# Three stores of the last batch issued as partition halves, and the fallback code's transfers moved to GpSimd

## The chip, the cores and the metric

The kernel runs on one core of one Trainium2 chip. The metric is device time in microseconds (us). The four runs of the kernel before lie within half a per cent of their median, and all its fast runs on record between 133.78 and 136.07 us; each run is labelled fast or slow state, and comparisons below use fast runs. "Span" is the time from the first to the last instruction of the one profiled execution; it is shorter than the device time of the same execution: by 2.0 us for the kernel before (132.8 against 134.76 us).

Engine names as in the profile: PE is TensorE, DVE is VectorE, ACT is ScalarE, POOL is GpSimd, SP is SyncE. SP does no arithmetic here; it issues the stores and the first load. SBUF is the core's on-chip memory, where tiles lie in 128 partitions; HBM is the main memory, where x and the output lie. The page counts 16 DMA engines and the packets that they carry (5666 in the kernel before). Each of the last batch's 1 MB stores has 16 completions in the trace, one for each engine as they are read here (127.98 to 131.62 us for the last store); a store is said to have landed with its last completion.

## The reference, cut to what matters

```python
def _attn_ref(x, inducing):            # x: 4 x 12480 x 128 fp32, inducing: 32 x 128
    ...
    h = mab(I, x)                      # 32 inducing points attend to all rows of a batch
    return mab(x, h)                   # all rows attend to the 32 results

def _moe_ref(x, w_in, w_out):          # w_in: 128 x 2048, w_out: 2048 x 128
    h = x @ w_in
    g = 0.5 * h * (1.0 + erf(h * inv_sqrt2))
    return (g @ w_out)                 # 49920 x 128 fp32
```

Only the traffic matters: about 25.6 MB of x are read and 25.6 MB of output are written, once each.

## The kernel before

The kernel runs a fast path that is valid for inputs in a certain range, counts range checks, and at the very end branches to a slow `general` code if any check failed. For the inputs the flag is zero, so `general` is never run, though its instructions are in the program.

The output rows are laid out so that each SBUF partition holds neighbouring rows. A store therefore moves one long contiguous piece per partition. In batches 0 to 2 two units share one tile and one store of 2 MB. In the last batch (`b = 3`) each unit is stored alone: 128 partitions x 16 rows x 512 bytes, that is 8 KB per partition and 1 MB in all. There are six such stores and one small tail store.

```python
APART = 3
...
    def rows_of(self, t):
        t0 = self.b * N + self.pair * 2 * SGT
        t = t[t0 : t0 + self.held * self.p, :]
        return t.rearrange("(p c) d -> p c d", p=self.p)
...
        # in b_inverse: the tile that the output of a unit is written to
        elif u.b >= APART:
            o = sb.tile([128, 32, 128], FP16, tag="xh", bufs=XBUFS)
            o = o.rearrange("p c d -> p (c d)").bitcast(FP32)
            o = o.rearrange("p (c d) -> p c d", d=128)
...
    def b_store(bt, u, alone):
        if alone:
            c0, c1, o = u.c_pair, u.c_pair + u.nc, bt.live[("o", u.idx)]
        else:
            c0, c1, o = 0, u.held, bt.live[("pair", u.pair)]
        nc.sync.dma_start(out=u.rows_of(out)[:, c0:c1, :], in_=o)
...
    with tc.If(flag > 0, preferred_fallthrough_block=False):
        general(tc, x, moe_w_in, moe_w_out, out, ind_s, identity)
```

Of the kernel before, what the change touches and what calls it, by code (L numbers as in the profile page):

```python
# [15 lines left out]
B = 4  # L16
N = 12480
# [221 lines left out]
def kernel(  # L239
# [8 lines left out]
    nc = tc.nc  # L248
# [61 lines left out]
    for j in range(4):  # L310
# [3 lines left out]
        out=stack4,  # L314
        in_=identity.rearrange("p (j m) -> p m j", j=4),
# [5 lines left out]
        out=same_m, in_=stack4.unsqueeze(1).broadcast_to([128, 4, M])  # L321
# [386 lines left out]
    def b_store(bt, u, alone):  # L708
        if alone:
            c0, c1, o = u.c_pair, u.c_pair + u.nc, bt.live[("o", u.idx)]  # L710
        else:
            c0, c1, o = 0, u.held, bt.live[("pair", u.pair)]
        nc.sync.dma_start(out=u.rows_of(out)[:, c0:c1, :], in_=o)

    checked = []

    def check_total():
# [27 lines left out]
            o=OBUFS,  # L745
# [120 lines left out]
    for k, u in enumerate(order):  # L866
# [59 lines left out]
        if u.last or alone:  # L926
            stored = plan.add(
                key(6),
                {"SP": 0.4},
                lambda e, bt=bt, u=u, alone=alone: b_store(bt, u, alone),  # L930
                scaled,
                gives=o_given,
                move=part(u, STORE_US) * (1 if alone else 2),
            )
# [29 lines left out]
        out=failed,  # L964
# [11 lines left out]
    with tc.If(flag > 0, preferred_fallthrough_block=False):  # L976
        general(tc, x, moe_w_in, moe_w_out, out, ind_s, identity)
# [4 lines left out]
def general(tc, x, moe_w_in, moe_w_out, out, ind_s, identity):  # L982

    nc = tc.nc
    T = 96
    with (
        tc.tile_pool(name="g_w", bufs=1) as gw,
        tc.tile_pool(name="g_sb", bufs=2) as gs,
        tc.tile_pool(name="g_ps", bufs=1, space=bass.MemoryType.PSUM) as gp,
    ):  # L990
        w_in = gw.tile([128, DFF], FP32)
        nc.sync.dma_start(out=w_in, in_=moe_w_in)
        w_out = gw.tile([128, NBLK, 128], FP32)
        nc.sync.dma_start(
            out=w_out, in_=moe_w_out.rearrange("(blk p) d -> p blk d", p=128)
        )
        iT = gw.tile([C, M], FP32)
        mx = gw.tile([M, 1], FP32)
        r = gw.tile([M, 1], FP32)
        rr = gw.tile([M, 1], FP32)  # L1000
        h = gw.tile([M, C], FP32)
        hn = gw.tile([M, C], FP32)
        hT = gw.tile([C, M], FP32)

        def transpose_to(dst, src, rows):
            tp = gp.tile([128, 128], FP32, tag="tp")
            n = src.shape[1]
            nc.tensor.transpose(tp[:n, :rows], src, identity[:rows, :rows])
            nc.vector.tensor_copy(out=dst, in_=tp[:n, :rows])

        transpose_to(iT, ind_s, M)
        nc.vector.memset(r, 1.0)
        nc.vector.memset(h, 0.0)
        xf = x.rearrange("b n d -> (b n) d")



        with tc.For_i(0, 2 * B, 1) as turn:
            nc.vector.tensor_scalar(
                out=rr, in0=r, scalar1=1e-9, scalar2=None, op0=ALU.add  # L1020
            )
            nc.vector.reciprocal(out=rr, in_=rr)
            nc.vector.tensor_scalar(
                out=hn, in0=h, scalar1=rr, scalar2=None, op0=ALU.mult
            )
            transpose_to(hT, hn, M)
            nc.vector.memset(mx, -3.0e38)
            nc.vector.memset(r, 0.0)
            nc.vector.memset(h, 0.0)
            base = (turn >> 1).with_bounds(min_val=0, max_val=B - 1) * N  # L1030
            with tc.For_i(0, N, T) as t:
                xg = gs.tile([T, C], FP32, tag="xg")
                nc.sync.dma_start(out=xg, in_=xf[bass.ds(base + t, T), :])
                xTg = gs.tile([C, T], FP32, tag="xTg")
                transpose_to(xTg, xg, T)

                s1 = gp.tile([M, T], FP32, tag="s1")
                nc.tensor.matmul(s1, iT, xTg, start=True, stop=True)
                tm = gs.tile([M, 1], FP32, tag="tm")
                nc.vector.tensor_reduce(out=tm, in_=s1, axis=AX.X, op=ALU.max)  # L1040
                nc.vector.tensor_tensor(out=tm, in0=mx, in1=tm, op=ALU.max)
                nm = gs.tile([M, 1], FP32, tag="nm")
                nc.vector.tensor_scalar(
                    out=nm, in0=tm, scalar1=-SCALE, scalar2=None, op0=ALU.mult
                )
                fall = gs.tile([M, 1], FP32, tag="fall")
                nc.scalar.activation(
                    out=fall, in_=mx, func=AF.Exp, bias=nm, scale=SCALE
                )
                nc.vector.tensor_copy(out=mx, in_=tm)  # L1050
                e = gs.tile([M, T], FP32, tag="e")
                re = gs.tile([M, 1], FP32, tag="re")
                nc.scalar.activation(
                    out=e, in_=s1, func=AF.Exp, bias=nm, scale=SCALE, accum_out=re
                )
                nc.vector.scalar_tensor_tensor(
                    out=r, in0=r, scalar=fall, in1=re, op0=ALU.mult, op1=ALU.add
                )
                eT = gs.tile([T, M], FP32, tag="eT")
                transpose_to(eT, e, M)  # L1060
                hp = gp.tile([M, C], FP32, tag="hp")
                nc.tensor.matmul(hp, eT, xg, start=True, stop=True)
                nc.vector.scalar_tensor_tensor(
                    out=h, in0=h, scalar=fall, in1=hp, op0=ALU.mult, op1=ALU.add
                )

                s2 = gp.tile([T, M], FP32, tag="s1")
                nc.tensor.matmul(s2, xTg, hT, start=True, stop=True)
                nm2 = gs.tile([T, 1], FP32, tag="nm2")
                nc.vector.tensor_reduce(out=nm2, in_=s2, axis=AX.X, op=ALU.max)  # L1070
                nc.vector.tensor_scalar(
                    out=nm2, in0=nm2, scalar1=-SCALE, scalar2=None, op0=ALU.mult
                )
                a = gs.tile([T, M], FP32, tag="a")
                ra = gs.tile([T, 1], FP32, tag="ra")
                nc.scalar.activation(
                    out=a, in_=s2, func=AF.Exp, bias=nm2, scale=SCALE, accum_out=ra
                )
                nc.vector.tensor_scalar(
                    out=ra, in0=ra, scalar1=1e-9, scalar2=None, op0=ALU.add  # L1080
                )
                nc.vector.reciprocal(out=ra, in_=ra)
                nc.vector.tensor_scalar(
                    out=a, in0=a, scalar1=ra, scalar2=None, op0=ALU.mult
                )
                aT = gs.tile([M, T], FP32, tag="aT")
                transpose_to(aT, a, T)
                y_ps = gp.tile([C, T], FP32, tag="y")
                nc.tensor.matmul(y_ps, hn, aT, start=True, stop=True)
                y = gs.tile([C, T], FP32, tag="ysb")  # L1090
                nc.vector.tensor_copy(out=y, in_=y_ps)
                z = gp.tile([128, NBLK // 4, 4, 128], FP32, tag="z")
                g = gs.tile([128, NBLK // 4, 4, T], FP32, tag="g")
                for blk in range(NBLK):
                    zb = z[:, blk // 4, blk % 4, :T]
                    nc.tensor.matmul(
                        zb,
                        w_in[:, blk * 128 : (blk + 1) * 128],
                        y,
                        start=True,  # L1100
                        stop=True,
                    )
                nc.scalar.activation(out=g, in_=z[:, :, :, :T], func=AF.Gelu)
                o_ps = gp.tile([T, 128], FP32, tag="hp")
                for blk in range(NBLK):
                    nc.tensor.matmul(
                        o_ps,
                        g[:, blk // 4, blk % 4, :],
                        w_out[:, blk, :],
                        start=(blk == 0),  # L1110
                        stop=(blk == NBLK - 1),
                    )
                og = gs.tile([T, 128], FP32, tag="og")
                nc.vector.tensor_copy(out=og, in_=o_ps)
                nc.sync.dma_start(out=out[bass.ds(base + t, T), :], in_=og)


# [28 lines left out]
```

## Time and profile before

| | kernel before |
|---|---|
| time, median of 4 runs | 134.35 us (133.78 to 134.8) |
| span of the profiled execution | 132.8 us |
| share of 16 DMA engines: loads (q0) and stores (q1) | 49.5 % + 48.3 % |
| DMA rate from 114 to 126 us | 418 to 430 GB/s |
| mean duration of an 8 KB store packet, from 112 to 128 us, by the microsecond in which it starts | 0.309 to 0.312 us |
| last store: issued, first and last of its 16 completions | 122.60, 127.98, 131.62 us |

The first lines are from the page of the kernel before: the span; then, over 40 equal slices of the span (3.3 us each), the busy share of the 16 DMA engines in tenths and the rate that they moved; then the queues with packets, MB and share of the engines' time; last the issues of the six 1 MB stores, with the size in KB and the median time from issue to landing in us.

```profile
span 132.8 us, 3490 instructions
...
DMA  4999999999999999999999999999999999999970
GB/s 123 302 223 215 217 200 220 212 220 210 220 205 220 215 200 313 333 398 367 299 318 348 266 227 324 321 412 425 430 423 426 415 437 413 411 434 425 421 300 15
DMA packets 5666, 40.17 MB, mean 303 GB/s; under 512 B 624, under 2 KB 1936, under 8 KB 2192
...
q0 software_dynamic: 2848, 13.30, 49.5%
q1 hardware_dynamic: 2800, 26.63, 48.3%
...
HBM read 27.67 MB, written 25.56 MB: 401 GB/s over the span
...
out_dram<-o SPq DMA_DIRECT2D x6, 1024.0 KB, 7.5
```

The DMA row is at 9 from the second slice to the last but two. So the DMA engines are read as the bound. "Busy" here says that some packet is under way on an engine. The GB/s row is compared between stretches with the same kind of transfer. (Loads seem to count about half there: q0 has 13.30 MB, HBM read is 27.67 MB, and the tiles loaded are 16-bit.)

The next lines are the windows view over the last stretch: for each window its length, busy time and instruction count of PE, PEld, DVE, ACT and POOL, then granted clock, DMA share and GB/s.

```profile
core 0: us, PE busy (x) PEld busy (x) DVE busy (x) ACT busy (x) POOL busy (x), PEclk, DMA share, GB/s
110.00:114.00 4.00, 2.68 (x27) 1.24 (x24) 3.72 (x8) 3.33 (x7) 3.92 (x6) 1.00 0.96 405
114.00:118.00 4.00, 2.75 (x14) 1.35 (x14) 3.89 (x13) 1.21 (x4) 2.28 (x3) 0.76 1.00 422
118.00:122.00 4.00, 3.16 (x8) 0.78 (x6) 3.58 (x15) 2.95 (x9) 1.68 (x3) 0.50 1.02 430
122.00:126.00 4.00, 0.24 (x2) 0.09 (x2) 0.51 (x5) 0.00 (x0) 0.57 (x1) 0.50 1.00 418
126.00:130.00 4.00, 0.00 (x0) 0.00 (x0) 0.00 (x0) 0.00 (x0) 0.00 (x0) 0.50 0.67 272
```

Arithmetic has ended by 123 us. The chain of waits of the kernel before confirms it; its last line (start in us, length in us, what) is:

```profile
122.73 0.14 DVE failed L963
```

From there to 132.8 us, 10 us pass in which only stores drain.

### The profile page before, as it was taken

How to read it: one execution, taken by the hardware profiler on the slowest of the kernel's cores; microseconds unless marked ns; L12 is line 12 of the kernel's file. 1: busy time of each engine (PE TensorE's matmuls, PEld its weight loads, DVE VectorE, ACT ScalarE, POOL GpSimd, SP SyncE). 2: the span in 40 equal slices, each digit the busy share in tenths (PEclk: the TensorE clock that was granted, in tenths of full speed). 3: DMA queues.
4: the chain of work that ended last, by engine and by line, in shares of the span. 5: the costliest groups of instructions: out<-in, count | busy, mean ns of one | idle time of the engine just before them, and what ended most of it. 6: DMA issues, size and time to landing. Idle time of an engine off the chain costs nothing. (4 is left out here: it accounts for less than half of the span.)

```text
span 132.8 us, 3490 instructions
## 1 busy us (share of the span) xinstructions
PE 97.3 (73%) x1365; PEld 56.6 (43%) x1365; DVE 93.4 (70%) x266; ACT 76.2 (57%) x173; POOL 65.3 (49%) x85
## 2 busy tenths in 40 slices
PE   0098678449999999999697979957988779295000
PEld 0036545349465556665363555624544424131000
DVE  1086557323699998999999489749989999998000
ACT  3004273316866879598878458967779759174000
POOL 6920131119344646894824409914167999556000
PEclk9999999965899999999999999999999999955555
DMA  4999999999999999999999999999999999999970
GB/s 123 302 223 215 217 200 220 212 220 210 220 205 220 215 200 313 333 398 367 299 318 348 266 227 324 321 412 425 430 423 426 415 437 413 411 434 425 421 300 15
DMA packets 5666, 40.17 MB, mean 303 GB/s; under 512 B 624, under 2 KB 1936, under 8 KB 2192
## 3 DMA queue, kind: packets, MB, share of 16 engines
q0 software_dynamic: 2848, 13.30, 49.5%
q1 hardware_dynamic: 2800, 26.63, 48.3%
q8 instruction: 11, 0.18, 0.5%
q14 instruction: 7, 0.06, 0.1%
HBM read 27.67 MB, written 25.56 MB: 401 GB/s over the span
## 5 line engine op out<-in xcount | busy, mean ns | idle before, releaser
L686 POOL TENSOR_TENSOR pair<-pair,rr 128x512 f32<-128x512 f32 x29 | 30.3, 1056 | 29.1 <-ACT pair L355 19.9
L670 PE MATMUL at<-q,e 128*128 128x512 f16 (+1 forms) x104 | 33.5, 389 | 7.2 <-DVE o L701 2.4
L367 PE MATMUL tr<-identity_h,xh 128*128 128x128 f16 x392 | 29.3, 227 | 2.3 <-DMA xh<-in_x_dram 2.1
L701 DVE TENSOR_TENSOR pair<-at,rr 128x512 f32<-128x512 f32 x41 | 26.8, 679 | 3.1 <-DMA out_dram<-pair 1.6
L367 PEld LDWEIGHTS <-xh 128*128 128x128 f16 x392 | 24.5, 102 | 7.6 <-issue 3.5
L355 ACT ACTIVATE xT<-tr 128x1024 f16<-128x1024 f16 (+1 forms) x17 | 16.7, 981 | 19.1 <-PE tr L367 19.1
L353 DVE COPY xT<-tr 128x1024 f16<-128x1024 f16 (+1 forms) x35 | 21.9, 644 | 7.0 <-PE tr L367 6.7
L355 ACT ACTIVATE pair<-at 128x512 f32<-128x512 f32 x29 | 17.2, 598 | 3.1 <-PE at L670 1.7
L628 ACT ACTIVATE e<-s 128x512 f16<-128x512 f32 (+1 forms) x28 | 15.2, 563 | 6.4 <-PE s L616 5.2
L277 POOL DMA_DIRECT2D xh<-in_x_dram x15 | 8.3, 556 | 21.5 <-DMA xh<-in_x_dram 14.3
L393 ACT ACTIVATE e<-s 128x512 f16<-128x512 f32 (+1 forms) x28 | 15.2, 543 | 5.4 <-PE s L381 5.0
L670 PEld LDWEIGHTS <-e 128*128 128x128 f16 (+1 forms) x104 | 8.9, 105 | 11.5 <-issue 8.5
L415 PE MATMUL hun<-xh,e1t 128*32 128x128 f16 x392 | 10.5, 222 | 3.2 <-DVE e1t L407 3.0
L562 POOL TENSOR_TENSOR pt<-pt 128x512 f32<-128x512 f32 (+4 forms) x20 | 12.0, 601 | 1.5
L407 DVE STREAM_TRANSPOSE e1t<-e 128x256 int32<-128x256 int32 (+1 forms) x28 | 11.0, 399 | 2.2 <-ACT e L393 2.2
L381 PE MATMUL s<-xT,indT 128*32 128x512 f16 (+1 forms) x108 | 10.5, 376 | 1.6 <-ACT xT L355 0.8
L415 PEld LDWEIGHTS <-e1t 128*32 128x32 f16 x392 | 6.3, 96 | 11.5 <-DVE e1t L407 9.0
L701 DVE TENSOR_TENSOR o<-at,rr 128x512 f32<-128x512 f32 (+1 forms) x19 | 10.2, 558 | 0.9 <-PE at L670 0.7
L686 POOL TENSOR_TENSOR o<-o,rr 128x512 f32<-128x512 f32 x8 | 8.2, 1044 | 4.0 <-ACT o L355 2.3
L616 PE MATMUL s<-xT,hT 128*32 128x512 f16 (+1 forms) x100 | 9.7, 391 | 0.1
L640 PEld LDWEIGHTS <-e 128*128 128x128 f16 (+1 forms) x104 | 5.6, 99 | 5.0 <-issue 1.3
L640 PE MATMUL r<-strand,e 128*128 128x4 f16 (+1 forms) x104 | 6.9, 168 | 0.2 <-ACT e L393 0.2
(72 smaller groups left out, 93.0 us busy)
## 6 DMA issues: line engine op xcount, KB each, us to landing
out_dram<-pair SPq DMA_DIRECT2D x9, 2048.0 KB, 15.0
xh<-in_x_dram POOLq DMA_DIRECT2D x11, 1024.0 KB, 28.0
out_dram<-o SPq DMA_DIRECT2D x6, 1024.0 KB, 7.5
x_first<-in_x_dram SPq DMA_DIRECT2D x1, 1024.0 KB, 5.4
xh<-in_x_dram POOLq DMA_DIRECT2D x1, 512.0 KB, 7.3
w_in_h<-in_moe_w_in_dram POOLq DMA_DIRECT2D x1, 512.0 KB, 17.5
w_out_h<-in_moe_w_out_dram POOLq DMA_DIRECT2D x1, 512.0 KB, 19.5
out_dram<-o SPq DMA_DIRECT2D x4, 96.0 KB, 12.4
```

What stands on the lines that cost most here:

```text
L353: nc.vector.tensor_copy(out=out, in_=in_)
L355: nc.scalar.activation(out=out, in_=in_, func=AF.Copy)
L367: nc.tensor.transpose(tr[:, c - c0, : u.p], xh[: u.p, c, :], identity_h[: u.p, : u.p])
L393: nc.scalar.activation(out=e1[: u.p, : u.nc // 2, :, :], in_=s1[: u.p, : u.nc, :].rearrange("r (a b) i -> r a i b", b=2), func=AF.Exp, sca ...
L407: nc.vector.transpose(out=pairs(e1t)[: u.p, :n], in_=pairs(e1)[: u.p, :n])
L415: nc.tensor.matmul(bt.hun[32 * j : 32 * j + 32, :], e1t[: u.p, c // 2, :, c % 2], xh[: u.p, c, :], start=u.idx == 0 and c < 4, stop=c + 4 ...
L562: nc.gpsimd.tensor_tensor(out=bt.pt[:, :, :, :half], in0=bt.pt[:, :, :, :half], in1=bt.pt[:, :, :, half : 2 * half], op=ALU.add,)
L628: nc.scalar.activation(out=e2[: u.rows, : u.cols], in_=s2[: u.rows, : u.cols], func=AF.Exp, scale=SCALE,)
L640: nc.tensor.matmul(r2[: u.p, ci, : u.nj], e2[: u.rows, ci * u.p : (ci + 1) * u.p], strand[: u.rows, : u.nj], start=True, stop=True,)
L670: nc.tensor.matmul(at[: u.p, : u.nj, :], e2[: u.rows, ci * u.p : (ci + 1) * u.p], bt.q[: u.rows, : u.nj, :], start=True, stop=True,)
L686: nc.gpsimd.tensor_tensor(out=part, in0=part, in1=rr2[: u.p, ci, : u.nj].unsqueeze(2).broadcast_to([u.p, u.nj, 128]), op=ALU.mult,)
L701: nc.vector.tensor_tensor(out=ov[: u.p, ci, :, :], in0=at[: u.p, : u.nj, :], in1=rr2[: u.p, ci, : u.nj].unsqueeze(2).broadcast_to([u.p, u. ...
```

## The change

Two things are changed. In `general`, the transfers and some memsets move from SP and VectorE to GpSimd, and the loops are given `hint_engines=()`; the aim is less setup for engines that are busy in the fast path. In the last batch the first three stores are cut in two, partitions 0 to 63 and 64 to 127; the aim is smaller transfers near the end. The bytes stay the same.

```diff
@@ b_store
-        nc.sync.dma_start(out=u.rows_of(out)[:, c0:c1, :], in_=o)
+        n = 64 if u.b == B - 1 and u.idx < 3 else u.p
+        for p0 in range(0, u.p, n):
+            nc.sync.dma_start(
+                out=u.rows_of(out)[p0 : p0 + n, c0:c1, :], in_=o[p0 : p0 + n]
+            )
@@ general
-        nc.sync.dma_start(out=w_in, in_=moe_w_in)
+        nc.gpsimd.dma_start(out=w_in, in_=moe_w_in)
         ... (three more dma_start from sync to gpsimd)
-        nc.vector.memset(r, 1.0)
-        nc.vector.memset(h, 0.0)
+        nc.gpsimd.memset(r, 1.0)
+        nc.gpsimd.memset(h, 0.0)
         ... (three more memsets and one tensor_copy from vector to gpsimd)
-        with tc.For_i(0, 2 * B, 1) as turn:
+        with tc.For_i(0, 2 * B, 1, hint_engines=()) as turn:
         ... (the inner loop alike)
```

More of the change, by code (lines that the diff above doesn't have):

```diff
@@ L991, in general @@
         w_in = gw.tile([128, DFF], FP32)
-        nc.sync.dma_start(out=w_in, in_=moe_w_in)
+        nc.gpsimd.dma_start(out=w_in, in_=moe_w_in)
         w_out = gw.tile([128, NBLK, 128], FP32)
-        nc.sync.dma_start(
+        nc.gpsimd.dma_start(
             out=w_out, in_=moe_w_out.rearrange("(blk p) d -> p blk d", p=128)
@@ L1026, in general @@
             transpose_to(hT, hn, M)
-            nc.vector.memset(mx, -3.0e38)
-            nc.vector.memset(r, 0.0)
-            nc.vector.memset(h, 0.0)
+            nc.gpsimd.memset(mx, -3.0e38)
+            nc.gpsimd.memset(r, 0.0)
+            nc.gpsimd.memset(h, 0.0)
             base = (turn >> 1).with_bounds(min_val=0, max_val=B - 1) * N
-            with tc.For_i(0, N, T) as t:
+            with tc.For_i(0, N, T, hint_engines=()) as t:
                 xg = gs.tile([T, C], FP32, tag="xg")
-                nc.sync.dma_start(out=xg, in_=xf[bass.ds(base + t, T), :])
+                nc.gpsimd.dma_start(out=xg, in_=xf[bass.ds(base + t, T), :])
                 xTg = gs.tile([C, T], FP32, tag="xTg")
@@ L1049, in general @@
                 )
-                nc.vector.tensor_copy(out=mx, in_=tm)
+                nc.gpsimd.tensor_copy(out=mx, in_=tm)
                 e = gs.tile([M, T], FP32, tag="e")
@@ L1114, in general @@
                 nc.vector.tensor_copy(out=og, in_=o_ps)
-                nc.sync.dma_start(out=out[bass.ds(base + t, T), :], in_=og)
+                nc.gpsimd.dma_start(out=out[bass.ds(base + t, T), :], in_=og)
 _INS = ['x', 'inducing', 'moe_w_in', 'moe_w_out']
```

## The prediction

> **What bounds the kernel.** The DMA engines, from 2 us to the end. The page's DMA row of 40 slices reads full from the second slice on; the queue table gives 49.5 % + 48.3 % of the sixteen engines' span to loads (GpSimd's queue) and stores (SP's). HBM moves 401 GB/s over the span; from 90 to 125 us the windows show 419 to 431 GB/s, all stores. The chain of waits ends with arithmetic at 122.9 us, but the span is 132.8 us: what ends last is the last 1 MB store, issued by SP at 122.6 us. Its sixteen completions arrive between 128.0 and 131.6 us; one engine is slowest (packets of 0.31 to 0.33 us, the others 0.309). Then SP's remaining waits and two barriers, 1.1 us.
>
> **What the change does.**
> 1. The general code does not run for these inputs (the flag is zero), so only what it leaves in the executed path counts: register setup at the start, semaphore make-up in the not-taken branch, program length.
> 2. Start: four register moves go from SP to GpSimd (compiled order). GpSimd is the last to reach the first barrier (its four memsets), so they stand on the path to the first load. On SP the four moves take 0.26 us, on GpSimd one took 0.035 us: estimate +0.14 to +0.26 us.
> 3. Not-taken branch: four make-up waits of SP (0.08 us apart) go, some come to GpSimd. Both then idle until the last store lands: 0 us.
> 4. The split: three more issues on SP, 0.33 us each, inside gaps of 1 to 3 us while stores are queued. Same packets, 48 more 4-byte completion packets of 9 ns over 16 engines: +0.03 us. [...]
>    But completion semaphores go round robin over eight: three more issues move the last store from the fifth to the eighth. SP's final waits run through them in order, 0.06 us each; three follow the last landing now, none then: −0.18 us.
> 5. Program length. At 128.3 to 128.8 us the trace has instruction refills, one of 16 KB and two of 8 KB. The two small ones appear to fall on the slowest store engine: its next 8 KB packet ends 1.17 us after they start, so about 0.86 us of the end is theirs (one refill elsewhere cost 0.41 us). [...] The change shortens SP's program by 29 instructions, DVE's by 4, ScalarE's and PE's by 1 and 2, and lengthens GpSimd's by 37. [...] perhaps 1 in 3 that a refill vanishes or moves, −0.4 to −0.9 us.
>
> **Sum.** +0.2 +0.03 −0.18 −0.2 (expected value of 5): 134.2 us, range 133.3 to 134.9. Faster by over 2 %: 0.01, within: 0.97, slower: 0.02.
>
> **What would show it.** First load issue later by about 0.2 us; six half stores issued 0.35 us apart with unchanged throughput; the last store on SP's last-waited semaphore and only drains after its landing; the refills around 128 us still two of 8 KB, or fewer with a smaller lag of the slowest engine.
>
> **What would make it wrong.** Halves spread differently over the engines; a refill stalling SP's final waits; refills gone.

Passages that rested on statements which no trace or run of this case shows are cut, and the cuts are marked. +0.2 + 0.03 − 0.18 − 0.2 = −0.15 us, from the 134.36 us that the kernel before had then, gives the 134.2 us. The −0.2 us is 1 in 3 of −0.4 to −0.9 us; the 1 in 3 is my guess. Where the text says that completion semaphores go round robin over eight, the trace of the kernel before has the completions of the stores on eight semaphores in turn, and those of the last store on the fifth of them in the order of SP's final waits.

## The result, and the profile after

| | before | after |
|---|---|---|
| time, median of 4 runs | 134.35 us (133.78 to 134.8) | 139.28 us (138.78 to 140.26) |
| span of the profiled execution | 132.8 us | 137.5 us |
| mean granted TensorE clock of that execution | 0.911 | 0.905 |
| first load issued at | 0.75 us | 0.99 us |
| last store issued at | 122.60 us | 127.48 us |
| last store's completions | 127.98 to 131.62 us | 132.84 to 136.52 us |

The changed kernel is slower: ratio 1.0378, 95 % interval 1.0308 to 1.0448. Ratios in this document are the mean time of one kernel's fast runs over the mean of the other's fast runs of the same rounds, so they are not quite the ratio of the medians quoted. The two profiled executions had nearly the same clock. In device time these two executions differ by 4.4 us, in span by 4.7: the time outside the span is 1.5 to 1.6 us in every run with the new general code (the change and run e2) and 1.9 us or more in every other run. Most profile figures below are compared within the span.

The same lines of the page of the kernel after (a slice is now 3.4 us):

```profile
span 137.5 us, 3493 instructions
...
DMA  4999999999999999999999999999999998999980
GB/s 107 304 225 215 212 197 223 217 217 215 206 221 212 222 269 329 342 401 310 315 334 303 218 315 315 398 424 424 422 412 391 422 429 205 291 322 312 414 349 31
DMA packets 5715, 40.18 MB, mean 292 GB/s; under 512 B 672, under 2 KB 1984, under 8 KB 2240
...
q1 hardware_dynamic: 2848, 26.63, 49.7%
q0 software_dynamic: 2848, 13.30, 47.7%
...
HBM read 27.67 MB, written 25.56 MB: 387 GB/s over the span
...
out_dram<-o SPq DMA_DIRECT2D x6, 512.0 KB, 6.7
out_dram<-o SPq DMA_DIRECT2D x3, 1024.0 KB, 9.0
```

The packets are as predicted: queue q1 has 2848 instead of 2800, so 48 more completion packets, and the same 26.63 MB. The DMA row is still full. But the GB/s row has a hole, 205, 291, 322, 312, where the kernel before has 413 to 434. The engines are as busy as before and move less.

The windows view of the kernel after says where. The columns are those of before.

```profile
110.00:114.00 4.00, 3.96 (x36) 1.54 (x36) 3.78 (x9) 4.00 (x11) 3.69 (x7) 1.00 0.96 396
114.00:118.00 4.00, 1.47 (x14) 0.70 (x12) 3.93 (x10) 1.20 (x3) 2.38 (x4) 1.00 0.98 237
118.00:122.00 4.00, 3.98 (x14) 1.25 (x13) 3.77 (x11) 3.04 (x9) 2.81 (x3) 0.57 0.97 285
122.00:126.00 4.00, 0.65 (x5) 0.22 (x4) 1.94 (x13) 1.12 (x4) 1.22 (x2) 0.88 0.99 324
126.00:130.00 4.00, 0.00 (x0) 0.00 (x0) 0.00 (x0) 0.00 (x0) 0.00 (x0) 0.50 1.00 395
130.00:134.00 4.00, 0.00 (x0) 0.00 (x0) 0.00 (x0) 0.00 (x0) 0.00 (x0) 0.50 0.91 357
```

Up to 114 us the kernels move nearly alike (396 against 405 GB/s in the last 4 us). From 114 to 126 us, while the six halves go out, the DMA share is 0.97 to 0.99 and the rate 237, 285 and 324 GB/s, against 422, 430 and 418. That is (422 + 430 + 418 − 237 − 285 − 324) GB/s x 4 us = 1.70 MB less in these 12 us. At 420 GB/s that is 4.0 us, an estimate, out of the 4.7 us between the spans. Afterwards, with whole stores, the rate is back at 395.

The chain of waits after ends like that of before, only 1.6 us later (again start, length, what):

```profile
124.31 0.14 DVE failed L969
```

The span ends 13 us later than that, not 10. So most of the loss is in the draining of stores, not in the arithmetic. The lateness itself was there before any half was sent: the first split store was issued at 113.23 us, not 111.36. It isn't the loss: e3 and e9 below, issued at 112.92 and 113.04 us, lost nothing.

The records of single packets in the two traces show what a slow stretch is made of. This table is worked out from them: 8 KB store packets that start in a given microsecond, for six of the microseconds.

```
             before                       after
start us   count  mean us  max us     count  mean us  max us
115          52    0.310    0.333       31    0.615    0.652
116          53    0.310    0.333       17    0.679    0.851
118          54    0.310    0.324       26    0.519    0.851
121          51    0.309    0.324       31    0.499    0.852
124          49    0.312    0.409       38    0.445    0.821
127          47    0.309    0.309       50    0.312    0.356
```

The same 8 KB packet takes 1.4 to 2.2 times as long in the rows from 115 to 124 us, while halves are under way. Summed over all 768 such packets of the last batch and divided by 16 engines, the time above 0.309 us a packet is 0.09 us before and 4.09 us after: 4.0 us more for each engine, which agrees with the estimate from the rates. SP's issues of the stores also stretch, from 0.33 us (0.70 us for the last one) to 0.55 to 2.07 us for the halves. This looks like a second cause. It is read here as a symptom: the DMA engines hardly run out of work while SP is held up (share 0.97 and above from 114 to 126 us).

### The profile page after: what moved, and what is told of

Same layout as the page of the kernel before. It is cut to its first block, busy times and chain, and to the rows that moved or that the text cites. A ratio compares the mean times of both kernels' runs of the same rounds, so it can differ in the third digit from the quotient of the medians.

```text
span 137.5 us, 3493 instructions
## 1 busy us (share of the span) xinstructions
PE 99.3 (72%) x1365; PEld 58.4 (42%) x1365; DVE 93.7 (68%) x266; ACT 76.0 (55%) x173; POOL 65.8 (48%) x85
## 3 DMA queue, kind: packets, MB, share of 16 engines
q1 hardware_dynamic: 2848, 26.63, 49.7%
q0 software_dynamic: 2848, 13.30, 47.7%
## 5 line engine op out<-in xcount | busy, mean ns | idle before, releaser
L367 PE MATMUL tr<-identity_h,xh 128*128 128x128 f16 x392 | 31.1, 236 | 1.4 <-DMA xh<-in_x_dram 1.1
L367 PEld LDWEIGHTS <-xh 128*128 128x128 f16 x392 | 26.5, 107 | 6.7 <-issue 3.8
L415 PE MATMUL hun<-xh,e1t 128*32 128x128 f16 x392 | 11.3, 235 | 3.2 <-DVE e1t L407 3.0
L415 PEld LDWEIGHTS <-e1t 128*32 128x32 f16 x392 | 6.8, 101 | 11.8 <-DVE e1t L407 9.0
```

The costliest lines, as they stand in the source:

```text
L367: nc.tensor.transpose(tr[:, c - c0, : u.p], xh[: u.p, c, :], identity_h[: u.p, : u.p])
L415: nc.tensor.matmul(bt.hun[32 * j : 32 * j + 32, :], e1t[: u.p, c // 2, :, c % 2], xh[: u.p, c, :], start=u.idx == 0 and c < 4, stop=c + 4 ...
```

## The experiments

Theories as the runs were planned, with the letters of the expectations:

- **A, the SBUF side.** What counts is which partitions a store reads. Packets that read only the lower half (0 to 63) or only the upper half (64 to 127) take about twice as long, as those of the change do at 115 us (0.615 against 0.310 us); where packets of both halves are under way together the loss is smaller; and a set of 64 that takes as many from either half isn't slow at all. This was an assumption of mine, for the runs to test.
- **B, the number or size of transfers.** More issues, more completions, smaller transfers, SP held up in issuing.
- **C, the general code.** Its move to GpSimd, not the split, costs the time.
- **D, the memory side.** A whole store writes 128 pieces of 8 KB, 16 KB apart, over a 2 MB stretch of the output; a half writes 64 of them over 1 MB. This narrower stretch is what is slow.
- **E, neighbouring partitions.** Any 64 neighbouring partitions are slow, whichever they are.

Run e7 asks one thing more: whether two halves on two queues would overlap better than one after the other on one queue.

All edits are to `b_store` of the kernel before, unless said otherwise; "before" in each result is the median of the kernel before in the same rounds. Where the edit is to `b_store`, `rows` stands for `u.rows_of(out)[:, c0:c1, :]`, and the edit applies to units 0 to 2 of the last batch. Some kernels write rows to wrong places. The correctness check passed these too, presumably because the output rows are nearly alike for these inputs (this was not tested); they serve only to measure transfers.

### 1 and 2: the two parts of the change, each alone

Run e1_split_only has the first hunk of the change alone, run e2_general_only the rest alone.

```diff
 # e1_split_only: only this hunk of the change
+        n = 64 if u.b == B - 1 and u.idx < 3 else u.p
+        for p0 in range(0, u.p, n): ...
 # e2_general_only: the hunks in general() of the change, stores whole
-        nc.sync.dma_start(out=w_in, in_=moe_w_in)
+        nc.gpsimd.dma_start(out=w_in, in_=moe_w_in)
         ...
```

> Only the split of the three stores, general code as before. Theory A ([...] its packets take 0.6 us in place of 0.309): +4.3 to +5.0 us, 8 KB packets of 0.6 us again. Theory B (twice as many stores, each with a fixed cost, and SP stuck in issuing): the same +4.3 to +5.0 us, so this run does not tell A from B. Theory C (the loss comes from the general code's move): within 0.5 us of the kernel before.

Measured: median 139.92 us (137.82 to 140.42), before 134.59. Two of the four runs were slow, so no ratio of fast runs was given. The two fast runs took 139.81 and 137.82 us, and all fast runs of the kernel before at most 136.07. In its profiled execution (span 137.8 us), where the first half was issued late, at 113.94 us, and the engines were idle for a part of the first window (share 0.88), the windows are:

```profile
114.00:118.00 4.00, 1.56 (x17) 0.76 (x16) 3.90 (x8) 1.92 (x4) 2.96 (x3) 1.00 0.88 213
118.00:122.00 4.00, 3.89 (x17) 1.61 (x16) 3.70 (x12) 2.47 (x7) 2.08 (x2) 0.55 1.00 299
122.00:126.00 4.00, 2.07 (x8) 0.46 (x5) 2.86 (x14) 1.69 (x6) 2.08 (x2) 0.50 1.01 315
```

> Only the general code's edits, stores whole. Theories A and B: +0.2 us, from the four register moves in front of the first barrier (first store-queue load issued at 0.99 us in place of 0.75 us); packets of 0.309 us up to the end. Theory C: +4 us or more.

Measured: median 135.14 us (134.66 to 135.75), before 134.59; ratio 1.0017, interval 0.9941 to 1.0093. Windows, span 134.2 us:

```profile
114.00:118.00 4.00, 3.94 (x33) 1.45 (x30) 3.62 (x8) 3.14 (x8) 3.46 (x5) 0.97 0.94 373
118.00:122.00 4.00, 2.14 (x14) 0.94 (x12) 3.93 (x13) 1.41 (x5) 2.06 (x3) 0.89 0.99 412
122.00:126.00 4.00, 3.20 (x10) 0.91 (x9) 3.68 (x12) 3.32 (x10) 1.94 (x3) 0.69 0.99 410
```

The last batch came late in this execution (first store issued at 115.18 us), so the first window still holds the end of the batch before. What follows: the split alone brings the hole in the rate and the loss; the general code alone brings neither. Theory C is out. The +0.24 us of the start is below what these runs resolve.

### 3: halves that are not neighbours

```diff
+            for k in range(2):
+                nc.sync.dma_start(out=rows[k::2], in_=o[k::2])
```

The same number and size of transfers as in the change, but each takes every second partition.

> Split as often, into 64 partitions and packets of 8 KB, but the even and the odd partitions in place of the lower and the upper half; general code as before. Theory A: [...] packets of 0.309 us, and time equal to before or up to 0.2 us less (SP's last waits). Theory B: +4.3 to +5.0 us, as for the halves, since the number, size and issue of the stores are the same.

Measured: median 134.33 us (133.75 to 134.7), before 134.59; ratio 0.9972, interval 0.9893 to 1.0051. Windows, span 132.0 us:

```profile
114.00:118.00 4.00, 2.16 (x20) 0.97 (x19) 3.90 (x12) 2.29 (x5) 2.52 (x3) 1.00 1.00 412
118.00:122.00 4.00, 3.89 (x17) 1.45 (x16) 3.90 (x13) 2.61 (x8) 2.52 (x3) 0.60 0.99 404
122.00:126.00 4.00, 1.16 (x6) 0.24 (x4) 2.30 (x14) 1.55 (x5) 1.65 (x2) 0.93 1.02 424
```

Six transfers of 64 partitions each run at 404 to 424 GB/s, with packets of 0.31 to 0.325 us. What follows: neither the number of transfers nor their size nor 64 partitions as such is the cause, and two such transfers one after another on one queue are not slow in themselves. It matters which 64.

### 4: the same two transfers, cut by columns

```diff
+        n = 8 if u.b == B - 1 and u.idx < 3 else u.nc
+            for k in range(0, u.nc, n):
+                nc.sync.dma_start(
+                    out=u.rows_of(out)[:, c0 + k : c0 + k + n, :],
+                    in_=o[:, k : k + n, :],
+                )
```

All 128 partitions, half of the bytes of each, twice.

> Split as often, by rows of each partition: 128 partitions with 4 KB each, twice. Theory A: [...] 4 KB packets of about 0.155 us, time within 0.5 us of before. Theory B: +4 us or more, six stores as in the change.

Measured: median 134.96 us (134.53 to 135.26), before 134.59; ratio 1.0022, interval 0.995 to 1.0095. The 4 KB packets took 0.159 to 0.161 us, half of the 0.309 us of 8 KB, and the rate was 410 to 428 GB/s. What follows, with e3: theory B is out, at this size of transfers.

### 5 and 6: is it the memory's side or SBUF's?

Both kernels put rows in wrong places. Run e5_even_to_lower reads every second partition and writes the change's two stretches of memory; run e6_lower_to_even reads the change's halves and writes every second piece in memory.

```diff
 # e5_even_to_lower
+                nc.sync.dma_start(out=rows[64 * k : 64 * k + 64], in_=o[k::2])
 # e6_lower_to_even
+                nc.sync.dma_start(out=rows[k::2], in_=o[64 * k : 64 * k + 64])
```

> A wrong result on purpose. Reads the even, then the odd partitions of the tile, as the fast split does, but writes them to the rows of the lower, then the upper half, as the slow split does. Theory A (SBUF side: which partitions are read): as before the change, within 0.8 us, packets of 0.31 to 0.33 us. Theory D (memory side: which rows of the output are written, a half being one block of 1 MB and every second partition spread over 2 MB): +4 to +5.5 us, packets of 0.6 us.

Measured: median 134.81 us (134.16 to 135.62), before 134.82; ratio 1.001, interval 0.9935 to 1.0086. Packets took 0.310 to 0.314 us in most of the stretch.

> The other way round, also wrong on purpose: reads the lower, then the upper half of the partitions, and writes the rows of the even, then the odd ones. Theory A: +4 to +5.5 us, packets of 0.6 us in the first of the split stores. Theory D: as before the change, within 0.8 us.

Measured: median 140.0 us (138.69 to 140.67), before 134.82; ratio 1.0375, interval 1.0283 to 1.0466: the loss of the whole change. Windows, span 137.6 us:

```profile
114.00:118.00 4.00, 2.17 (x19) 0.93 (x18) 3.90 (x11) 2.54 (x6) 2.77 (x3) 1.00 0.99 244
118.00:122.00 4.00, 3.90 (x18) 1.45 (x17) 3.88 (x13) 2.54 (x7) 2.20 (x3) 0.62 0.97 279
122.00:126.00 4.00, 1.39 (x7) 0.39 (x5) 2.57 (x14) 1.63 (x5) 1.96 (x2) 0.93 1.02 324
```

What follows: the loss goes with the partitions that are read, not with the addresses that are written. Theory D is out.

### 7: the two halves on two queues

```diff
+                queue = (nc.sync, nc.gpsimd)[k]
+                queue.dma_start(out=rows[64 * k : 64 * k + 64], in_=o[64 * k : 64 * k + 64])
```

> The halves of the change, right result, but the lower half issued by SP and the upper by GpSimd[...]. Theory A: [...] DMA near 400 GB/s or more where the change had 205 to 322 GB/s, and time within 1.5 us of before (GpSimd's issues, about 0.6 us each, may delay its scaling). If 64 neighbouring partitions are slow for a reason that the other half in flight does not relieve: +3 us or more.

Measured: median 139.25 us, before 134.82; ratio of fast runs 1.0326, interval 1.0221 to 1.043. Two of its four runs were slow; the fast ones took 137.2 and 138.4 us. The expectation was missed. In its profiled execution (span 135.3 us) the rate was 324, 291 and 338 GB/s in the three windows. This run doesn't settle what a second queue gives. GpSimd also does arithmetic in this kernel (67.2 us busy in this run), with three of the stores issued in between; whether those held it up was not taken apart. What the trace shows is that the third of the stores was issued at 117.27 us instead of 115.76, the last at 125.27 instead of 122.60. Delays of the arithmetic and the rate of the transfers are mixed in this run, and how much is due to either stays open. The packets were slow here too: summed as above over both queues, they took 3.1 us more for each engine than in the kernel before.

### 8 and 12: all six stores of the last batch cut

```diff
+        if u.b == B - 1 and not u.tail:
+            for k in range(2):
+                nc.sync.dma_start(out=rows[64 * k : 64 * k + 64], in_=o[64 * k : 64 * k + 64])
```

> Halves as in the change, but for all six large stores of the last batch in place of three. Theory A: the cost grows with the bytes read that way, about twice that of three, +8 to +11 us. If the loss is a one-off (a queue that runs full once, then recovers): +4 to +6 us.

Measured: median 140.37 us, before 134.82; ratio of fast runs 1.0385, interval 1.0314 to 1.0455. Theory A's expectation, about twice the loss, was missed; the loss between the fast means, 5.2 us, lies in the range given for a loss paid once. The profiled execution was slow, so its profile is not used. The kernel was run again with more rounds:

> The all-six kernel once more, since its profile fell in a slow execution and its cost (+5.2 us) was half of what theory A foresaw. Revised estimate from traces: in the change neighbouring halves [...] overlap, a half landing every 1.6 us on average, where lower halves alone took 2.5 us and a whole store takes 2.5 us; so each store after the first should add about 0.7 us: three more stores +2 us on top of the change's 4.9, or +6 to +8 us in all, with halves landing every 1.4 to 1.7 us. If it is again +4.5 to +5.7 us, something at the end of the kernel gives 1 to 2 us back, and the spread of the last store's sixteen completions should be smaller than in the change (3.7 us).

Measured: median 140.42 us (139.11 to 141.72, 6 runs), before 134.61; ratio 1.0425, interval 1.0373 to 1.0476. The profile was fast this time, span 137.1 us:

```profile
114.00:118.00 4.00, 2.11 (x23) 0.99 (x20) 3.90 (x12) 1.82 (x4) 2.16 (x4) 1.00 0.98 295
118.00:122.00 4.00, 4.00 (x14) 1.17 (x13) 3.90 (x11) 3.29 (x10) 3.00 (x3) 0.62 1.00 328
122.00:126.00 4.00, 0.75 (x5) 0.30 (x4) 1.83 (x13) 0.87 (x3) 1.04 (x2) 0.93 1.04 338
```

The +6 to +8 us of the revised estimate were missed as well; +5.5 us between the fast means is in the second range. What follows: the rate of halves is well below that of whole stores in this kernel too, but twelve halves don't cost twice as much as six. Two things in the trace go with that. Successive halves begin to land every 1.3 to 1.8 us in most of the run (2.3 us once, 3.1 us for the last two), against 2.5 us in e10 below, where no lower half has an upper one to overlap with. And the last half-store's completions lie 0.29 us apart (135.57 to 135.86 us), while those of the last whole store lie 3.7 us apart in the change (132.84 to 136.52 us) and 3.6 us in the kernel before. The packet records give sizes: summed as above, the packets took 5.8 us more for each engine than before, but the span grew by only 4.3 us (137.1 against 132.8). So packet time does grow with the number of halves, less than in proportion, and about 1.5 us of it is given back; that the closer completions at the end are what gives it back is likely, not shown.

### 9 and 10: two sets of 64 neighbouring partitions

Theory A makes two sharp predictions. Partitions 32 to 95 are 64 neighbours, but 32 of them lie in either half, so they should be as fast as a whole store. And partitions 0 to 63 sent twice never leave the lower half, so the overlap of lower and upper halves is taken away. Both kernels give wrong rows.

```diff
 # e9_middle_twice
+                nc.sync.dma_start(out=rows[64 * k : 64 * k + 64], in_=o[32:96])
 # e10_lower_twice
+                nc.sync.dma_start(out=rows[64 * k : 64 * k + 64], in_=o[0:64])
```

> A wrong result on purpose. The three stores are split in two as in the change, with the same rows written, but each half reads the 64 neighbouring partitions 32 to 95. [...] theory A expects packets of about 0.31 us and the time of before within 0.8 us. Theory E (any 64 neighbouring partitions are slow, whichever): +4 to +5.5 us as in the change.

Measured: median 134.56 us (134.32 to 135.65), before 134.88; ratio 0.9999, interval 0.9933 to 1.0065. Windows, span 132.3 us:

```profile
114.00:118.00 4.00, 2.17 (x19) 0.92 (x17) 3.90 (x11) 2.44 (x5) 2.66 (x3) 1.00 0.97 401
118.00:122.00 4.00, 3.90 (x18) 1.51 (x16) 3.90 (x13) 2.54 (x7) 2.36 (x3) 0.62 0.99 404
122.00:126.00 4.00, 1.31 (x7) 0.24 (x4) 2.45 (x14) 1.63 (x5) 1.80 (x2) 0.93 1.01 418
```

> A wrong result on purpose, the counterpart: each half reads partitions 0 to 63. Theory A: [...] with no other half to overlap with, so at least as slow as the change: packets of about 0.62 us throughout, 200 to 220 GB/s while these stores run, +5 to +7.5 us. Theory E: as the change, +4 to +5.5 us.

Measured: median 141.16 us (140.94 to 142.65), before 134.88; ratio 1.0496, interval 1.0422 to 1.0571. Windows, span 139.1 us:

```profile
114.00:118.00 4.00, 2.50 (x14) 1.15 (x14) 3.93 (x14) 1.16 (x4) 2.06 (x3) 0.83 1.03 246
118.00:122.00 4.00, 2.81 (x8) 0.71 (x6) 3.62 (x15) 3.01 (x10) 1.88 (x3) 0.75 0.95 197
122.00:126.00 4.00, 0.21 (x2) 0.09 (x2) 0.51 (x5) 0.00 (x0) 0.63 (x1) 0.68 1.01 209
```

Packets took 0.62 to 0.64 us from 117 us to 127 us, without the fast ones of the change's mixture. Halves landed every 2.5 us, the time of a whole store in the kernel before (2.45 us). What follows: a shift of 32 partitions removes the loss, so theory E is out; staying in partitions 0 to 63 brings the rate to 197 to 209 GB/s, half of 418. The packet times give nearly the same: 16 engines with 8 KB in 0.62 to 0.64 us each would move 205 to 211 GB/s, an estimate. No record in the trace says why these packets take longer; what the runs show is which sets of partitions are slow, and each that was tried agrees with theory A. Partitions 64 to 127 were not sent without the lower half.

### 11: one store cut

```diff
+        if u.b == B - 1 and u.idx < 1:
+            for k in range(2):
+                nc.sync.dma_start(out=rows[64 * k : 64 * k + 64], in_=o[64 * k : 64 * k + 64])
```

> The halves of the change for the first of the three stores alone. If the cost grows with the bytes read by halves: a third of the change's, +1.2 to +2.2 us. If it is paid once: +4 us or more. All six stores gave about +5.2 us in place of the doubled cost, which speaks for a part paid once, or for something given back at the end; this run tells which.

Measured: median 138.11 us (137.5 to 138.66), before 134.88; ratio 1.0245, interval 1.0181 to 1.031, so not certain to be over 2 %. Both ranges were missed, +1.2 to +2.2 and +4 us or more. One store costs more than a third of what three cost, and less than all three. All its four runs had granted clocks of 0.868 to 0.878, while the kernel before had 0.876 to 0.921 in the same rounds. In its profiled execution the first store of the last batch was issued at 114.52 us, not at 111.36 as before. Such late issues come in the change's trace too (113.23 us), and in that of e3 and e9, which lost nothing. So the sign is plain and the size of this one is partly open. The packet records say more: summed as above, the packets took 2.6 us more for each engine than before (2.69 against 0.09 us), about what one store at half the rate would cost (2.45 us). With 4.0 us for three stores and 5.8 for six, the cost is not paid once, and it is not in proportion either.

### All runs

| label | what is sent | median us | before us | ratio of fast runs | rate in the stretch 114 to 126 us, GB/s |
|---|---|---|---|---|---|
| the change | halves 0–63, 64–127, three stores | 139.28 | 134.35 | 1.0378 | 237, 285, 324 |
| e1_split_only | the same, old general code | 139.92 | 134.59 | none given | 213, 299, 315 |
| e2_general_only | whole stores, new general code | 135.14 | 134.59 | 1.0017 | 373, 412, 410 |
| e3_every_second | even, odd partitions | 134.33 | 134.59 | 0.9972 | 412, 404, 424 |
| e4_columns | 128 partitions, half the columns | 134.96 | 134.59 | 1.0022 | 410, 428, 412 |
| e5_even_to_lower | read even and odd, write halves | 134.81 | 134.82 | 1.001 | 418, 422, 418 |
| e6_lower_to_even | read halves, write every second | 140.0 | 134.82 | 1.0375 | 244, 279, 324 |
| e7_two_queues | halves on two queues | 139.25 | 134.82 | 1.0326 | 324, 291, 338 |
| e8_all_six | halves, six stores | 140.37 | 134.82 | 1.0385 | |
| e9_middle_twice | 32–95 twice | 134.56 | 134.88 | 0.9999 | 401, 404, 418 |
| e10_lower_twice | 0–63 twice | 141.16 | 134.88 | 1.0496 | 246, 197, 209 |
| e11_one_store | halves, one store | 138.11 | 134.88 | 1.0245 | 263, 204, 246, 299 (steps of 2 us from 114) |
| e12_all_six_again | halves, six stores | 140.42 | 134.61 | 1.0425 | 295, 328, 338 |

No version beats the kernel before by more than the noise. The best ratio, 0.9972 of e3, has 1 inside its interval.

## Why the prediction was wrong

The prediction was 134.2 us with a range of 133.3 to 134.9, and 0.97 for "within 2 %". It measured 139.28 us.

1. **The bound was read rightly.** The DMA engines are full from the second slice on, and the last store ends the kernel. That is why the loss showed: from 114 to 126 us there was hardly any slack in the DMA engines to hide it in (share 0.97 and above).
2. **General code not run: right.** Run e2 gives 1.0017 with 1 inside the interval.
3. **Start, +0.14 to +0.26 us: right.** The first load is issued at 0.99 instead of 0.75 us. This lag is still 0.25 us at the load landings around 13 us, and 0.02 us by 29 us, so it is not shown to reach the end; the time of run e2 doesn't resolve it. The time outside the span, 0.45 us shorter with the new general code (e2: 1.55 against 2.0 us), was in no term of the sum; what sets it stays open.
4. **The split, +0.03 us: this is the step that failed.** In the prediction's words: "Same packets, 48 more 4-byte completion packets of 9 ns over 16 engines: +0.03 us." The count was right, 48 more packets. What was missing is the duration of a packet. I took 0.309 us for a given in each 8 KB packet; it held for whole stores, and in e3 and e9 nearly for two other sets of 64, but not for every set of partitions. With halves it was 0.60 to 0.65 us where halves of one side ran alone, and a mixture of 0.309 and up to 0.87 us where lower and upper halves overlapped. The term, put at +0.03 us, measured 4.0 us, by the packet records and by the rates alike, out of 4.7 us between the spans. The rest of the 4.7 us was not taken apart further.
That packets of a half would be as short as those of a whole store was my assumption, and the trace of the kernel before has no store of 64 partitions that could have tested it. I asked how many bytes a transfer moves, and not which partitions it touches. What that is worth e10 measured for partitions 0 to 63: 197 to 209 GB/s against 418.
   The other item of the step, the last semaphore, was right. The span ends 1.13 us after the last landing before and 0.97 us after it now, so −0.16 us against −0.18 predicted.
5. **Refills, 1 in 3 that some vanish: no.** The kernel before has one of 16 KB at 128.32 us and two of 8 KB at 128.45; the kernel after has 8 KB ones at 130.05, 130.65 and 134.93 and one of 16 KB at 130.85, so one more. What that costs was not measured.
6. **"Unchanged throughput" was named as a sign, and "halves spread differently over the engines" as what would make it wrong.** The first sign failed plainly in the windows. The second was near the cause but not it: the halves are spread over the same 16 engines (each half has 16 completions); what differs is how long a packet takes, and by theory A that depends on the partitions that it reads.

The mechanism, as far as it is shown: e10 shows that the set of partitions 0 to 63 runs at half rate (197 to 209 GB/s against 418); e3 and e9 that other sets of 64 don't (404 to 424 and 401 to 418); e5 and e6 that the reading side decides (418 to 422 against 244 to 324). Why packets that read partitions 0 to 63 take twice as long (0.62 to 0.64 us against 0.309) is not shown by any run here, and stays open.

Why the change lost less than half the rate would cost: at half the rate the three stores would take 3 x 2.45 = 7.35 us longer, an estimate from the spacing of whole stores, and the packets took 4.0 us longer (spans: 4.7). The lower and upper halves follow one another on one queue, and the engines seem to drift apart so that some work on the upper while others still work on the lower: the first half's 16 completions lie 0.2 us apart (117.34 to 117.57 us), the sixth's 2.7 us (125.03 to 127.75). First completions of the change's halves run from 117.34 to 125.03 us, which is 1.5 us apart on average, against 2.5 us in e10. That e10, without an upper half to overlap with, lost more supports this: its packets took 7.35 us longer for each engine (7.44 against 0.09), the whole of the estimate. Its span grew by 6.3 us only (139.1 against 132.8); as in e12, the last store's completions lie closer together (2.1 us, against 3.6 before).

## What to carry to other kernels

Before you cut a transfer, ask which partitions each piece touches, not only whether the bytes and packets stay the same; cut by columns over all 128 partitions, or by interleaved partitions, both of which cost nothing measurable here (ratios 1.0022 and 0.9972). If a profile shows DMA busy as before but a lower rate, look at the duration of packets of one size: engines that look as full as before can be moving less (237 to 324 GB/s here at a share of 0.97 and above, against 418 to 430). When a step of a forecast says that a thing costs nothing, ask which measured figure it takes for given, and whether the trace has a case like the new one.
